# One core: W_in's low parts, token pieces and W_out's last block at other places of a scheduled three-layer kernel

## The chip, the cores and the metric

The kernel runs on one core of one Trainium2 chip, in one launch. The metric is the device time of one execution in microseconds (us). TensorE (PE) multiplies, VectorE (DVE), ScalarE (ACT) and GpSimd (POOL) prepare its operands and take up its results, and SyncE's queue (SP) issues every large transfer between HBM and the on-chip memory.

## The reference

Three stages, each feeding the next:

```python
# attention with decay, per head h of 8, batch 2, 768 tokens, head_dim 64
state = gamma * state + outer(k[t], v[t]);  y[t] = scale * q[t] @ state
# x = y as 1536 tokens x 512
# mixture: P from exp(x @ w_gate), 8 rounds of row and column normalization
for e in range(8): out += P[:, e:e+1] * (maximum(x @ w1[e], 0) @ w2[e])   # 512 -> 1024 -> 512
# dense layer on that output
h = x @ w_in;  g = maximum(h, 0) + alpha * minimum(h, 0);  y = g @ w_out   # 512 -> 2048 -> 512
```

## The kernel before, in words

**Phases.** After the attention, 20 phases follow, each one half of the tokens (768) with one expert or with one half of the dense layer's 2048 columns. Phases 0 to 7 are the first half's experts, 8 to 15 the second half's, 16 to 19 the dense layer (first half, columns' halves 0 and 1; second half, 1 and 0). In phases 8 to 19 ("fast", `FAST`) a phase is a list of 56 positions. Each position is one of the seven products of a Strassen scheme on one column block of four, and each is six matmuls of 384 columns: three for the first and three for the second half of the contraction. Positions 0 to 26 and 28 are nearly all layer 1 (x by W_in), the rest layer 2 (h by W_out). From position 27 on layer 2's products u = 0 to 27 follow.

**Three matmuls for one product.** Both operands stand as a high part (rounded to fp32r by ScalarE) and a low part (what the rounding lost, a subtraction). `mm3` (L313 to L315) multiplies high by high, high by low, low by high, in this order, and all accumulate in one bank. So the low part of an operand is wanted one matmul later than its high part.

**Where operands come from.** A block `n` of W_in (four for each phase, n = 4 * phase + j) is loaded raw from HBM (`w_load`, L124). POOL makes its four sums (`w1_sum`, L139). ScalarE makes the high part in three pieces a, c and b (`w1_high`, L162), VectorE the low part (`w1_low`, L172). The raw buffers are two: block n + 2 is loaded when block n's part b (at its low step) has been issued, which `w1_low` queues in `unkept`, to be issued two positions later. `w1_at` gives the positions of the adds and of the three high and low steps; its first numbers for blocks n + 4 and n + 5 belong to the phase after.
The hidden state of layer 2 has 14 parts (`hs`): for each, ScalarE writes the high part (L1072) and VectorE the low part (L1080, or L1050 with the relu, or L1052). Part k is first wanted at layer 2's product 2k.
W_out of a dense block is prepared once, one block in each of phases 8 to 15 (`dense_prep`): load `dr` (L270), high `dw` (L275), low (L279), sums on POOL (L289), high and low of the sums, stored to HBM (L298), from where `ws` pieces are loaded later (L1091).
The tokens of a half are kept as pieces `xs` in HBM (`x_keep`: a term on POOL, L374, the high part on ScalarE, L382, a low part on POOL, L386, a store, L389) and fetched (L394). x_keep(2, k) is the second half's tokens for the experts, x_keep(3, k) the second half's for the dense layer, made from `total`, the mixture's output.

**What sets the order.** `step(phase, position, fn)` appends a function that issues instructions behind that position's matmuls; a position of 60 or more means position - 60 of the next phase. Each engine runs its instructions in the order of issue, and waits for each of them to have its inputs; so a waiting instruction holds back everything behind it on its engine. SP's queue is one such order: a load that waits for a buffer holds back the loads behind it.

**Gathers.** POOL adds layer 2's results of a phase to `total` in the next one (L1130, eight per phase, at positions 2, 5, 8, 11 for phases 10 to 15; for phase 15 they run during phases 15 and 16).

Of the kernel before, what the change touches and what calls it, by code (L numbers as in the profile page):

```python
# [23 lines left out]
E, F = 8, 1024  # L24
# [5 lines left out]
NJ = NF // 2  # L30
# [17 lines left out]
def tile_kernel(ctx, tc, lead, qkT, kv, ctab, w_gate, w1, w2, w_in, w_out, alpha, out):  # L48
# [119 lines left out]
    def w1_low(n, part, eng):  # L168
        if n >= NJ * len(PHASES) or same(n) or n // NJ in AGAIN and part == "c":
            return  # L170
        lo, src, hi = ws1[n].pop(part)
        eng.tensor_tensor(out=lo, in0=src, in1=hi.bitcast(F32), op=ALU.subtract)  # L172
        if part == "b" and n not in (0, 2 * NJ * E - 2):
            if n < NJ * E:
                w_load(0, n + 2)
            else:
                unkept.append([2, w_load, 0, n + 2])
        if n < NJ * E and part != "a":
            unkept.append([2, w1_keep, n, part, hi, lo])
# [246 lines left out]
    with tc.manual_schedule():  # L426

        with ExitStack() as actx:
# [53 lines left out]
            pool, dve = nc.gpsimd, nc.vector  # L482
# [722 lines left out]
        pool, dve = nc.gpsimd, nc.vector  # L1205
# [20 lines left out]
        def step(ph, pos, *fns):  # L1226
            if pos >= 60:
                ph, pos = ph + 1, pos - 60
            for fn in fns:
                at(ph, seq[ph][pos], fn)  # L1230
# [20 lines left out]
        def w1_at(ph, m, add_eng, eng, adds, ah, al, ch, cl, bh, bl):  # L1251
            step(ph, adds, lambda: w1_adds(m, add_eng))
            for part, hi, lo in (("a", ah, al), ("c", ch, cl), ("b", bh, bl)):
                step(ph, hi, lambda part=part: w1_high(m, part))
                step(ph, lo, lambda part=part: w1_low(m, part, eng))
# [7 lines left out]
        xk, x3 = [], []  # L1263
        for ph in range(len(PHASES)):
# [28 lines left out]
            if fast:  # L1293
                w1_at(ph, n + 2, pool, dve, 0, 4, 5, 5, 7, 10, 11)
                w1_at(ph, n + 3, pool, dve, 5, 10, 12, 12, 14, 17, 18)
                w1_at(ph, n + 4, pool, dve, 28 if ph == 2 * E - 1 else 18, 36, 38, 39, 40, 42, 43)
                w1_at(
                    ph, n + 5, pool, dve, 36 if ph >= 2 * E else 28,
                    *((44, 51, 48, 53, 50, 55) if ph == 2 * E - 1 else (44, 45, 48, 49, 50, 52))
                )  # L1300
            else:
                if ph:
# [29 lines left out]
            if fast:  # L1332
# [6 lines left out]
                        step(ph, (2, 5, 8, 11)[q // 2], lambda m=q // 2, h=q % 2: gather(m, h))  # L1339
                if ph < 2 * E:  # L1340
                    step(ph, 0, lambda ph=ph: weight_load(ph))
                    for pos, fn in zip((6, 14, 24, 27, 40, 52), dense_prep(ph - E)):
                        step(ph, pos, fn)
                o = ph < 2 * E
                for pos, fn, jp in (
# [8 lines left out]
                    step(ph, lows[k], lambda ph=ph, k=k: hlow(ph, k))  # L1354
                for pos, jp in ((34 if o else 40, 0), (36 if o else 41, 1)):
                    step(ph, pos, lambda ph=ph, jp=jp: t4(ph, jp))
                if ph in (E + 1, E + 4):
                    step(ph, 0, lambda k=(ph - E - 1) // 3: xk.extend(x_keep(2, k, *x_load(2, k))))
                if ph == 2 * E:
                    for k in range(2):  # L1360
                        step(ph, 8 + k, lambda k=k: x3.append(x_keep(3, k, *x_copy(k, total))))
                    step(ph + 1, 39, lambda: new_x(3, B22, T4))
                    for i, keys in enumerate((
# [4 lines left out]
                    )):  # L1368
                        for q, to in enumerate(keys):
                            step(ph + to // 56, to % 56, lambda i=i, q=q: x3[i % 2][i // 2][q]())  # L1370
# [149 lines left out]
```

## Time and profile before

| | |
|---|---|
| median of 3 runs | 1263.19 us (1262.98 to 1263.47) |
| profiled execution | 1262.42 us |
| its span | 1260.3 us |
| TensorE busy | 1251.2 us, 99% of the span |
| VectorE, ScalarE, POOL busy | 1006.5, 653.0, 446.8 us |
| granted TensorE clock | 1.0 of full speed over the whole span |

The profiled execution is 0.8 us under the median, and 2.1 us of it lie around the span. Since TensorE is busy 99% of the span, the time can only be moved by the waits that remain between two of its matmuls. A fast phase without waits is 56 positions of six matmuls. The rows of a timeline say when an instruction started, how long it ran, its engine and line, and in brackets, for how long the engine had idled and what released it. A matmul of 384 columns is shown with some 0.33 us, and the starts of two that don't wait lie 0.17 us apart, since they overlap.

### The profile page before, as it was taken

How to read it: one execution, taken by the hardware profiler on the slowest of the kernel's cores; microseconds unless marked ns; L12 is line 12 of the kernel's file. 1: busy time of each engine (PE TensorE's matmuls, PEld its weight loads, DVE VectorE, ACT ScalarE, POOL GpSimd, SP SyncE). 2: the span in 40 equal slices, each digit the busy share in tenths (PEclk: the TensorE clock that was granted, in tenths of full speed). 3: DMA queues.
4: the chain of work that ended last, by engine and by line, in shares of the span. 5: the costliest groups of instructions: out<-in, count | busy, mean ns of one | idle time of the engine just before them, and what ended most of it. 6: DMA issues, size and time to landing. Idle time of an engine off the chain costs nothing.

```text
span 1260.3 us, 20491 instructions
## 1 busy us (share of the span) xinstructions
PE 1251.2 (99%) x7358; PEld 1189.4 (94%) x7358; DVE 1006.5 (80%) x1538; ACT 653.0 (52%) x1211; POOL 446.8 (35%) x408
## 2 busy tenths in 40 slices
PE   9999999999999999999999999999999999999998
PEld 7889999989898989899999999999999999999998
DVE  6677888888888888859696968787786999797866
ACT  5644534444444445456455454546464656655573
POOL 5733252526161616101033433142413464633110
PEclk9999999999999999999999999999999999999999
DMA  9884999999999999899988989898989976684616
GB/s 361 275 286 144 318 342 353 329 339 335 346 338 338 337 341 341 280 345 343 378 293 326 324 297 334 308 348 300 351 285 320 339 269 192 224 302 169 213 56 184
DMA packets 219990, 375.00 MB, mean 298 GB/s; under 512 B 15809, under 2 KB 133617, under 8 KB 219889
## 3 DMA queue, kind: packets, MB, share of 16 engines
q1 hardware_dynamic: 219888, 373.70, 87.0%
q8 instruction: 58, 0.95, 0.3%
q14 instruction: 44, 0.35, 0.1%
HBM read 240.97 MB, written 131.10 MB: 295 GB/s over the span
## 4 chain that ended last, share of the span: by engine, by line
PE 90%; DVE 6%; DMA 2%; issue 1%; ACT 1%; SPq 0%; DVEq 0%
PE B L314 7%; PE B L313 7%; PE B L315 7%; PE o L313 7%; PE o L315 7%; PE o L314 7%; PE A L313 6%; PE A L315 6%; PE A L314 6%; PE D L314 4%; PE D L315 4%; PE D L313 4%; PE E L315 4%; PE E L313 4%; PE E L314 4%; DVE hs L1080 1%
## 5 line engine op out<-in xcount | busy, mean ns | idle before, releaser
L1072 ACT ACTIVATE hs<-b 128x768 fp32r<-128x768 f32 x168 | 139.1, 841 | 65.5 <-DVE b L1046 22.4
L139 POOL TENSOR_TENSOR raw<-raw 128x256 f32<-128x256 f32 x128 | 124.9, 986 | 92.6 <-DMA raw<-wd 52.4
L1080 DVE TENSOR_TENSOR hs<-b,hs 128x768 fp32r<-128x768 f32 x120 | 122.8, 1028 | 14.9 <-ACT hs L1072 14.6
L246 POOL TENSOR_TENSOR pr<-pr 128x256 f32<-128x256 f32 x52 | 51.0, 982 | 188.7 <-ACT ex L872 62.7
L313 PE MATMUL A<-xh,W 128*128 128x384 f32 x320 | 107.8, 337 | 0.0
L315 PE MATMUL A<-xh,W 128*128 128x384 f32 x320 | 107.2, 335 | 0.0
L314 PE MATMUL A<-xl,W 128*128 128x384 f32 x320 | 107.0, 334 | 0.0
L162 ACT ACTIVATE W<-raw 128x512 fp32r<-128x512 f32 (+1 forms) x138 | 94.0, 695 | 19.2 <-DVE raw L139 19.2
L314 PE MATMUL B<-hs,ws 128*128 128x384 f32 x288 | 96.5, 335 | 2.4 <-DVE hs L1080 2.4
L313 PE MATMUL B<-hs,ws 128*128 128x384 f32 x288 | 96.3, 334 | 0.2 <-ACT W L162 0.2
L315 PE MATMUL B<-hs,ws 128*128 128x384 f32 x288 | 96.3, 334 | 0.0
L1130 POOL TENSOR_TENSOR total<-total,t 128x384 f32<-128x384 f32 x56 | 71.6, 1309 | 68.1 <-DVE t L1110 68.1
L979 DVE TENSOR_TENSOR b<-E,b 128x384 f32<-128x384 f32 x48 | 26.7, 556 | 84.2 <-ACT W L162 48.1
L386 POOL TENSOR_TENSOR xs<-b,xs 128x384 fp32r<-128x384 f32 x19 | 24.1, 1269 | 189.3 <-ACT xs L382 172.7
L313 PE MATMUL B<-xh,W 128*128 128x384 f32 x268 | 90.7, 338 | 0.0
L172 POOL TENSOR_TENSOR W<-raw,W 128x512 fp32r<-128x512 f32 (+1 forms) x49 | 76.1, 1566 | 40.0 <-PE B L315 22.9
L315 PE MATMUL B<-xh,W 128*128 128x384 f32 x268 | 89.7, 335 | 0.0
L314 PE MATMUL B<-xl,W 128*128 128x384 f32 x268 | 89.6, 334 | 0.0
L964 ACT ACTIVATE B<-A 128x384 f32<-128x384 f32 x48 | 22.8, 476 | 123.3 <-PE A L315 121.8
L289 POOL TENSOR_TENSOR dr<-dr 128x256 f32<-128x256 f32 x32 | 37.4, 1167 | 131.7 <-DVE dw L279 93.5
L172 DVE TENSOR_TENSOR W<-raw,W 128x512 fp32r<-128x512 f32 (+1 forms) x89 | 82.1, 939 | 1.1 <-ACT W L162 1.1
L313 PE MATMUL D<-xh,W 128*128 128x384 f32 x236 | 79.4, 336 | 0.0
(498 smaller groups left out, 3992.3 us busy)
## 6 DMA issues: line engine op xcount, KB each, us to landing
ws<-c SPq DMA_DIRECT2D x168, 512.0 KB, 5.8
raw<-in_w_dram SPq DMA_DIRECT2D x64, 512.0 KB, 5.6
c<-W SPq DMA_DIRECT2D x64, 384.0 KB, 6.6
W<-c SPq DMA_DIRECT2D x22, 768.0 KB, 7.7
pr<-in_w_dram SPq DMA_DIRECT2D x32, 512.0 KB, 6.0
c<-pw SPq DMA_DIRECT2D x32, 512.0 KB, 7.2
c<-pr SPq DMA_DIRECT2D x32, 512.0 KB, 7.8
raws<-in_w_dram SPq DMA_DIRECT2D x32, 384.0 KB, 6.3
```

The lines of the kernel that those rows point to most:

```text
L139: eng.tensor_tensor(out=out, in0=in0, in1=in1, op=op)
L162: nc.scalar.activation(out=hi, in_=src, func=AF.Copy)
L172: eng.tensor_tensor(out=lo, in0=src, in1=hi.bitcast(F32), op=ALU.subtract)
L246: eng.tensor_tensor(out=out, in0=in0, in1=in1, op=op)
L289: nc.gpsimd.tensor_tensor(out=out, in0=in0, in1=in1, op=op)
L313: nc.tensor.matmul(ps, ah, bh, start=first, stop=False, skip_group_check=True)
L314: nc.tensor.matmul(ps, ah, bl, start=False, stop=False, skip_group_check=True)
L315: nc.tensor.matmul(ps, alo, bh, start=False, stop=last, skip_group_check=True)
L979: nc.vector.tensor_tensor(out=dst, in0=src, in1=dst, op=ALU.add)
L1072: nc.scalar.activation(out=t[:, 0, :], in_=hsource(ph, k), func=func)
L1080: nc.vector.tensor_tensor(out=lo, in0=src, in1=hi.bitcast(F32), op=ALU.subtract)
L1130: eng.tensor_tensor(out=dst, in0=dst, in1=tt[m, h], op=ALU.add)
```

## The change

The full diff, of which the numbers are positions:

```diff
--- before.py
+++ after.py
@@ -170,7 +170,8 @@
             return
         lo, src, hi = ws1[n].pop(part)
         eng.tensor_tensor(out=lo, in0=src, in1=hi.bitcast(F32), op=ALU.subtract)
-        if part == "b" and n not in (0, 2 * NJ * E - 2):
+        last = "c" if n // NJ in (2 * E, 2 * E + 1) and n % NJ == 1 else "b"
+        if part == last and n not in (0, 2 * NJ * E - 2):
             if n < NJ * E:
                 w_load(0, n + 2)
             else:
@@ -1293,10 +1294,14 @@
             if fast:
                 w1_at(ph, n + 2, pool, dve, 0, 4, 5, 5, 7, 10, 11)
                 w1_at(ph, n + 3, pool, dve, 5, 10, 12, 12, 14, 17, 18)
-                w1_at(ph, n + 4, pool, dve, 28 if ph == 2 * E - 1 else 18, 36, 38, 39, 40, 42, 43)
+                late_lows = ph in (2 * E - 1, 2 * E)
                 w1_at(
-                    ph, n + 5, pool, dve, 36 if ph >= 2 * E else 28,
-                    *((44, 51, 48, 53, 50, 55) if ph == 2 * E - 1 else (44, 45, 48, 49, 50, 52))
+                    ph, n + 4, pool, dve, 28 if ph == 2 * E - 1 else 18,
+                    *((36, 51, 39, 52, 42, 53) if late_lows else (36, 38, 39, 40, 42, 43))
+                )
+                w1_at(
+                    ph, n + 5, pool, dve, 28,
+                    *((44, 55, 48, 60, 50, 54) if late_lows else (44, 45, 48, 49, 50, 52))
                 )
             else:
                 if ph:
@@ -1339,7 +1344,8 @@
                         step(ph, (2, 5, 8, 11)[q // 2], lambda m=q // 2, h=q % 2: gather(m, h))
                 if ph < 2 * E:
                     step(ph, 0, lambda ph=ph: weight_load(ph))
-                    for pos, fn in zip((6, 14, 24, 27, 40, 52), dense_prep(ph - E)):
+                    places = (6, 14, 24, 27, 40, 52) if ph < 2 * E - 1 else (2, 10, 18, 19, 36, 52)
+                    for pos, fn in zip(places, dense_prep(ph - E)):
                         step(ph, pos, fn)
                 o = ph < 2 * E
                 for pos, fn, jp in (
@@ -1354,17 +1360,18 @@
                     step(ph, lows[k], lambda ph=ph, k=k: hlow(ph, k))
                 for pos, jp in ((34 if o else 40, 0), (36 if o else 41, 1)):
                     step(ph, pos, lambda ph=ph, jp=jp: t4(ph, jp))
-                if ph in (E + 1, E + 4):
-                    step(ph, 0, lambda k=(ph - E - 1) // 3: xk.extend(x_keep(2, k, *x_load(2, k))))
+                if ph in (E + 1, E + 3):
+                    k = (ph - E) // 2
+                    step(ph, 40 * k, lambda k=k: xk.extend(x_keep(2, k, *x_load(2, k))))
                 if ph == 2 * E:
                     for k in range(2):
                         step(ph, 8 + k, lambda k=k: x3.append(x_keep(3, k, *x_copy(k, total))))
                     step(ph + 1, 39, lambda: new_x(3, B22, T4))
                     for i, keys in enumerate((
                         (16, 16, 17, 19), (17, 17, 17, 21), (38, 38, 39, 42), (42, 42, 43, 45),
-                        (44, 48, 49, 51), (50, 54, 55, 57), (54, 60, 61, 63), (60, 66, 67, 69),
-                        (66, 71, 72, 74), (70, 74, 75, 77), (97, 97, 98), (100, 100, 101),
-                        (96, 103, 104), (101, 107, 108),
+                        (44, 48, 49, 51), (52, 56, 57, 59), (57, 61, 62, 64), (61, 66, 67, 69),
+                        (66, 70, 71, 73), (69, 74, 75, 77), (106, 106, 107), (110, 110, 110),
+                        (107, 111, 112), (108, 113, 114),
                     )):
                         for q, to in enumerate(keys):
                             step(ph + to // 56, to % 56, lambda i=i, q=q: x3[i % 2][i // 2][q]())
```

In words: (1) In phases 15 and 16 the low parts of the next phase's first two W_in blocks (64, 65 and 68, 69) move behind layer 2's last low parts of h, to positions 51 to 55 and the next phase's position 0. (2) For blocks 65 and 69 the load of the block two further is now issued behind part c instead of b. (3) In phase 15 the steps of W_out's last block stand at 2, 10, 18, 19, 36, 52 instead of 6, 14, 24, 27, 40, 52. (4) The load of the second half's tokens, k = 1, moves from phase 12, position 0, to phase 11, position 40. (5) Most steps that make the second half's token pieces for the dense layer move some positions later, the last ones from phase 17, position 40 on to phase 17, position 50 on.

VectorE's order at the end of phase 15, before. `hs15_k` are the low parts of h, `W_144<-raw0_64` the low parts of W_in's block 64, `E2` and `t15` sums of layer 2's results, `dr7` the low part of W_out's last block:

```order
L1080 TENSOR_TENSOR hs15_8_10622<-b120_15_10309,hs15_8_10622 128x768
L1160 TENSOR_TENSOR E2_15_0_10640<-B2_15_0_10552,d2_15_0_10599 128x384
L172 TENSOR_TENSOR W_144<-raw0_64_10426,W_144 128x512
L1160 TENSOR_TENSOR E2_15_1_10656<-B2_15_1_10566,d2_15_1_10612 128x384
L1080 TENSOR_TENSOR hs15_9_10643<-b121_15_10475,hs15_9_10643 128x768
L172 TENSOR_TENSOR W_144<-raw0_64_10426,W_144 128x768
L1110 TENSOR_TENSOR t15_00_10685<-A2_15_0_10503,pb15_10216 128x384
L1050 SCALAR_TENSOR_TENSOR hs15_10_10677<-b220_15_10225,hs15_10_10677 128x768
L1110 TENSOR_TENSOR t15_10_10698<-A2_15_1_10535,pb15_10216 128x384
L172 TENSOR_TENSOR W_144<-raw0_64_10426,W_144 128x512
L1050 SCALAR_TENSOR_TENSOR hs15_11_10701<-b221_15_10391,hs15_11_10701 128x768
```

And there in the changed kernel, some rows further:

```order
L1081 TENSOR_TENSOR hs15_12_10736<-b210_15_10235,hs15_12_10736 128x768
L1111 TENSOR_TENSOR t15_01_10760<-E2_15_0_10641,pb15_10216 128x384
L1081 TENSOR_TENSOR hs15_13_10752<-b211_15_10375,hs15_13_10752 128x768
L1111 TENSOR_TENSOR t15_11_10770<-E2_15_1_10657,pb15_10216 128x384
L172 TENSOR_TENSOR W_144<-raw0_64_10431,W_144 128x512
L172 TENSOR_TENSOR W_144<-raw0_64_10431,W_144 128x768
L280 TENSOR_TENSOR dr7_10239<-dr7_10239,dw7_10325 128x1024
L172 TENSOR_TENSOR W_144<-raw0_64_10431,W_144 128x512
L1111 TENSOR_TENSOR t15_20_10797<-B2_15_0_10552,pb15_10216 128x384
L172 TENSOR_TENSOR W_144<-raw0_65_10437,W_144 128x512
L1111 TENSOR_TENSOR t15_30_10808<-B2_15_1_10566,pb15_10216 128x384
L172 TENSOR_TENSOR W_144<-raw0_65_10437,W_144 128x512
```

The three W_in rows that stood between `hs15_9` and `hs15_11` now stand behind `hs15_13`, all six of block 64 and 65 together with `dr7`.

SP's queue from the end of phase 16, before. `ws17` are pieces of W_out for phase 17, `raw0_70` and `raw0_71` blocks of W_in, `xc3<-xs3` stores of token pieces:

```order
L1091 DMA ws17_0_11345<-c2_9_121 128x2x512
L389 DMA xc3_123<-xs3_1_1_11315 128x2x384
L124 DMA raw0_70_11349<-wd0_6_131 128x1024
L1091 DMA ws17_1_11364<-c2_9_121 128x2x512
L1091 DMA ws17_2_11385<-c2_9_121 128x2x512
L1091 DMA ws17_3_11407<-c2_9_121 128x2x512
L389 DMA xc3_123<-xs3_0_4_11377 128x2x384
L1091 DMA ws17_4_11424<-c2_9_121 128x2x512
L124 DMA raw0_71_11436<-wd0_7_132 128x1024
L1091 DMA ws17_5_11444<-c2_9_121 128x2x512
```

And in the changed kernel:

```order
L1092 DMA ws17_0_11342<-c2_9_121 128x2x512
L390 DMA xc3_123<-xs3_1_1_11313 128x2x384
L1092 DMA ws17_1_11358<-c2_9_121 128x2x512
L1092 DMA ws17_2_11379<-c2_9_121 128x2x512
L1092 DMA ws17_3_11399<-c2_9_121 128x2x512
L390 DMA xc3_123<-xs3_0_4_11371 128x2x384
L1092 DMA ws17_4_11418<-c2_9_121 128x2x512
L1092 DMA ws17_5_11435<-c2_9_121 128x2x512
L124 DMA raw0_70_11439<-wd0_6_131 128x1024
L124 DMA raw0_71_11478<-wd0_7_132 128x1024
```

The load of `raw0_70` stood ahead of `ws17_1`, and stands now behind `ws17_5`.

POOL's order at the start of phase 17, before (`b0_3_0`, `ba_3_1` the token terms of L374, `xs3` their low parts, `raw0_70` the sums of a W_in block):

```order
L374 TENSOR_TENSOR ba_3_1_10936<-ba_3_1_10936 128x384
L374 TENSOR_TENSOR b0_3_0_10921<-b1_3_0_10922,b0_3_0_10921 128x384
L386 TENSOR_TENSOR xs3_1_4_11433<-ba_3_1_10936,xs3_1_4_11433 128x384
L139 TENSOR_TENSOR raw0_70_11349<-raw0_70_11349 128x256 x4
L374 TENSOR_TENSOR ba_3_1_10936<-bb_3_1_10937,ba_3_1_10936 128x384
L386 TENSOR_TENSOR xs3_0_5_11499<-b0_3_0_10921,xs3_0_5_11499 128x384
L139 TENSOR_TENSOR raw0_71_11436<-raw0_71_11436 128x256 x4
L374 TENSOR_TENSOR b0_3_0_10921<-b0_3_0_10921,b1_3_0_10922 128x384
```

And in the changed kernel:

```order
L375 TENSOR_TENSOR ba_3_1_10936<-ba_3_1_10936 128x384
L139 TENSOR_TENSOR raw0_70_11439<-raw0_70_11439 128x256 x4
L387 TENSOR_TENSOR xs3_1_4_11451<-ba_3_1_10936,xs3_1_4_11451 128x384
L375 TENSOR_TENSOR b0_3_0_10921<-b1_3_0_10922,b0_3_0_10921 128x384
L375 TENSOR_TENSOR ba_3_1_10936<-bb_3_1_10937,ba_3_1_10936 128x384
L139 TENSOR_TENSOR raw0_71_11478<-raw0_71_11478 128x256 x4
L387 TENSOR_TENSOR xs3_0_5_11510<-b0_3_0_10921,xs3_0_5_11510 128x384
L375 TENSOR_TENSOR b0_3_0_10921<-b0_3_0_10921,b1_3_0_10922 128x384
```

The sums of `raw0_70` and the wait for its load now stand ahead of `xs3_1_4` and of the term that `xs3_0_5` needs. In the kernel before they stood behind both.

## Rows read from the trace of the kernel before

**Rows 1.** PE's waits, whole span: operation and releaser: us in all, times, longest.

```profile
PE B L314 <- DVE hs L1080: 2.4, 3, 1.1
...
PE E L314 <- DVE hs L1050: 0.5, 1, 0.5
PE E L314 <- DVE hs L1052: 0.3, 1, 0.3
PE B L313 <- ACT W L162: 0.2, 1, 0.2
```

**Rows 2.** PE's timeline at the end of phase 16: start, us, engine, line, operation.

```profile
1074.53 0.33 PE L315 MATMUL E<-hs,ws 128*128 128x384 f32 x1
1074.71 0.34 PE L313 MATMUL B<-hs,ws 128*128 128x384 f32 x1
1076.15 0.45 PE L314 MATMUL B<-hs,ws 128*128 128x384 f32 x1 [1.11 <-DVE hs L1080]
```

**Rows 3.** Chain that ends at 803 us, in phase 12: start, us, what.

```profile
789.51 10.96 DMA dr<-wd
```

**Rows 4.** PE's timeline in phase 12.

```profile
801.58 0.34 PE L315 MATMUL D<-xh,W 128*128 128x384 f32 x1
801.99 0.45 PE L313 MATMUL E<-xh,W 128*128 128x384 f32 x1
```

**Rows 5.** VectorE's timeline at the end of phase 15.

```profile
1009.64 1.03 DVE L172 TENSOR_TENSOR W<-raw,W 128x512 fp32r<-128x512 f32 x1
1010.60 1.76 DVE L1050 SCALAR_TENSOR_TENSOR hs<-b,hs 128x768 fp32r<-128x768 f32 x1
```

**Rows 6.** VectorE's timeline in the middle of phase 15.

```profile
981.65 0.95 DVE L1080 TENSOR_TENSOR hs<-b,hs 128x768 fp32r<-128x768 f32 x1
...
988.23 2.43 DVE L1080 TENSOR_TENSOR hs<-b,hs 128x768 fp32r<-128x768 f32 x2
990.58 1.49 DVE L1046 TENSOR_TENSOR b<-b,b 128x768 f32<-128x768 f32 x1
```

**Rows 7.** POOL's timeline, phases 15 to 17.

```profile
986.28 4.97 POOL L289 TENSOR_TENSOR dr<-dr 128x256 f32<-128x256 f32 x4 [23.12 <-DMA xh<-xc]
...
1018.95 4.99 POOL L139 TENSOR_TENSOR raw<-raw 128x256 f32<-128x256 f32 x4
1023.89 4.38 POOL L1130 TENSOR_TENSOR total<-total,t 128x384 f32<-128x384 f32 x4
...
1081.37 3.06 POOL L139 TENSOR_TENSOR raw<-raw 128x256 f32<-128x256 f32 x4
```

**Rows 8.** PE's timeline: matmuls of phases 15, 16 and 17.

```profile
990.39 0.33 PE L314 MATMUL A<-hs,ws 128*128 128x384 f32 x1
...
1030.99 0.33 PE L313 MATMUL E<-xh,W 128*128 128x384 f32 x1
...
1091.72 0.33 PE L313 MATMUL E<-xh,W 128*128 128x384 f32 x1
```

**Rows 9.** DMA from 1008 to 1032 us: transfers, KB each, median us to landing.

```profile
raw<-wd SPq DMA_DIRECT2D x2, 512.0 KB, 4.5
...
c<-dr SPq DMA_DIRECT2D x1, 512.0 KB, 3.1
```

**Rows 10.** ACT's timeline at the starts of phases 16 and 17.

```profile
1028.13 0.58 ACT L935 ACTIVATE n<-A,sa 128x384 f32<-128x384 f32 x1 [0.41 <-PE A L315]
...
1029.12 0.48 ACT L964 ACTIVATE E<-B 128x384 f32<-128x384 f32 x1
...
1085.12 0.51 ACT L382 ACTIVATE xs<-b 128x384 fp32r<-128x384 f32 x1
...
1089.90 0.47 ACT L964 ACTIVATE E<-B 128x384 f32<-128x384 f32 x1
```

**Rows 11.** SP's timeline at the start of phase 17.

```profile
1080.45 0.36 SPq L1091 DMA_DIRECT2D ws<-c  x1
```

**Rows 12.** DMA from 1070 to 1090 us.

```profile
raw<-wd SPq DMA_DIRECT2D x2, 512.0 KB, 6.3
```

## The prediction, on record before the changed kernel ran

> **What bounds the kernel now.** I read the page's engine shares first, then the list of TensorE's waits, then the timelines of the engines around the few waits that it names. TensorE is busy for 99% of the span, at a granted clock of 1.0 (the 2.4 GHz level) in every slice, and the change leaves its matmuls and their order as they are. So the change is worth what it takes from, or adds to, the gaps between matmuls. The reader is to see how few gaps there are: behind VectorE's low parts of h three of 2.4 us together, one of 0.5 and one of 0.3, and behind ScalarE's W_in part one of 0.2 [rows 1]. The list counts a little less than a gap costs. At the end of phase 16 the starts lie 1.44 us apart, where 0.18 would do, so the gap costs about 1.26 there and is listed with 1.11; the matmul behind it starts late by another tenth [rows 2]. I add 0.27 to each listed gap for that.
>
> All these gaps are together 3.4 us listed, about 5 us with the additions. That is the most the change can win from them.
>
> **The change part by part.** Every sum is made against the profiled execution, 1262.42 us (span 1260.3 and 2.1 around it), which lies 0.8 us under the median of 1263.19; I add the difference that comes out to the median.
>
> (a) The token load moved from phase 12 to phase 11. In phase 12 the load of W_out's block is 10.96 us on its way [rows 3], behind the two token loads on the same queue. ScalarE then converts that block in front of the copy that TensorE's next product needs, and that product starts 0.41 us behind the one before instead of 0.18 [rows 4]; with the tenth behind it, 0.35. Without the two loads the block comes earlier: -0.4. If phase 11, position 40, is as crowded, nothing is won; it can't cost more than the same 0.4 there, so the bounds are -0.4 and +0.4.
>
> (b) W_out's last block earlier in phase 15. The load, the high and the low part stand before the product that needs anything of them; the load at position 2 is covered by the eight positions to 10. I take 0; if the load were as slow as in phase 12 (10.96 us against 8 positions of 1.04 us [rows 3]), ScalarE would stand for some 2.6 us, of which the copies behind it hide most; upper bound +0.8, an estimate.
>
> (c) Its sums at position 19 instead of 27. They hold POOL for 4.97 us from 986.28, and POOL's sums of W_in follow without a gap [rows 7]. They start when VectorE's low part of that block is done, and that moves from position 24 to 18, about 5 us. So POOL is now busy from some 981 on, over five more microseconds in which VectorE works on low parts that TensorE waits for next. A 768-wide VectorE operation took 0.95 us at 981.65, with POOL idle, and 1.49 at 990.58, with POOL busy [rows 6]. I count nine VectorE operations with both inputs in the on-chip memory that come to lie beside POOL, at 0.54 each: 4.9. Of this 1.2 comes back, since the low part of W_out's block (1.2 us) has left this place, and two low parts have slack of about 1.0 (the one that ends about 989.4 is needed at 990.39 [rows 6, 8]) and 0.8. That leaves +1.9. If only the operations as wide as in the row count, six of the nine, 3.2 - 1.2 - 1.8 leaves +0.2; if the slack is half, it is +2.8. I take 1.9, since the nine come from the order of the engine, one by one.
>
> (d) W_in's low parts of block 64 out of phase 15's second half. One of them, 1.03 us at 1009.64, stands right in front of a low part of h which itself takes 1.76 [rows 5]. TensorE's wait for it, and the next one, are the 0.5 and one of the three of L1080; the other two of these hold 1.3 together beside the longest, 1.1 [rows 1, 2], so 0.65. The 0.2 behind ScalarE lies there too. With 0.27 each: 0.77 + 0.92 + 0.47 = 2.2. VectorE has then only low parts and gathers to make: -2.2 (at best that, at worst 0 if POOL's collisions alone make them late).
>
> (e) The start of phase 16. The low parts now stand behind h's last low part, then the low part of W_out's block, then block 64's part b, and only then may block 66 be loaded. From the last of h's parts the five VectorE operations end about 1.1 us into phase 16 (4.6 us by the widths, begun 3.5 us before it; an estimate). Then the load takes 4.5 us by the median of this stretch [rows 9], POOL's sums 3.1 when alone [rows 7], and three of the four gathers behind them 3.3 (4.38 for four [rows 7]). ScalarE's sign step at 1028.13 needs the third gather's buffer, and the copy at 1029.12, which follows on the same engine, needs 1.5 us from there [rows 10]. 1.1 + 4.5 + 3.1 + 3.3 + 1.5 = 13.5 us into the phase. TensorE wants that copy at its twelfth position, 1030.99 [rows 8], 11.5 into the phase: +2.0. In the kernel before, POOL had the load in time: its sums begin at 1018.95 without a wait [rows 7]. Behind the waiting sums on POOL stand the gathers, and behind ScalarE's high part of that block the copies for the second column block: both engines wait in one place. With the fastest large transfer of this stretch, 3.1 [rows 9], it is +0.6; with the loads of the next phase, 6.3 [rows 12], and sums of 4.1 instead of 3.1, +4.8.
>
> The Trainium skill, page "DMA: Bandwidth & Descriptors", section "Anatomy of one DMA — SWDGE (gpsimd) path", gives 2.0 us and the bytes at 436 GB/s for one transfer: 3.2 us for 512 KB, an estimate. The stretch shows 4.5 for these loads, so the measurement decides; by the rule (e) would be +0.7 and (g) +0.1, nearly the fast rival below.
>
> (f) Blocks 68 and 69 likewise out of phase 16's second half: the longest wait, 1.1, and the 0.3 [rows 1, 2], with 0.27 each: 1.95, so -1.9. At worst 0.
>
> (g) The start of phase 17. The load of block 70 now stands behind the piece of W_out that SP issues at 1080.45, 0.2 us into the phase [rows 11], so it starts some 0.65 into it and lands 6.3 later [rows 12]. POOL's sums for it, 3.1 [rows 7], now stand ahead of a low token part (1.0) and of the term (1.0) that ScalarE's token step at 1085.12 needs; from there to the end of the copy at 1089.90 ScalarE needs some 2.7 of its own work [rows 10]. 0.65 + 6.3 + 3.1 + 2.0 + 2.7 = 14.7 into the phase, wanted at 11.5 (1091.72 [rows 8]): +3.2. With 3.1 for the load it is +0.1, with POOL's sums at 4.1 it is +4.3.
>
> (h) The last token pieces go behind the low parts of phase 17's end, so POOL is quiet beside these: the last of the three waits, 0.65 and 0.27: -0.9 (worst 0). They are due in phase 18 only.
>
> Sum: -0.4 + 0 + 1.9 - 2.2 + 2.0 - 1.9 + 3.2 - 0.9 = +1.7. The profiled execution would be 1264.1, the median 1264.9. A measurement of this kernel tells no change from a change below about 0.2%, 2.5 us, so this forecast is "no change".
>
> **The rivals.**
>
> Fast loads: the transfers land in 3.1 us. For it: that is what a 512 KB transfer in this stretch took [rows 9]. Against it: the loads of W_in themselves took 4.5 and 6.3 [rows 9, 12]. Then (e) is +0.6, (g) +0.1 and (c) at its lower end +0.2: -0.4 + 0.2 - 2.2 + 0.6 - 1.9 + 0.1 - 0.9 = -4.5, 1258.7.
>
> Slow loads: the loads of 66 and 70 take 6.3, and POOL's sums beside VectorE's low parts 4.1, so that (e) is +4.8 and (g) +4.3: -0.4 + 1.9 - 2.2 + 4.8 - 1.9 + 4.3 - 0.9 = +5.6, 1268.8. For it: sums of 4.99 at 1018.95 [rows 7], and the low parts moved to just this place. Against it: 4.5 in that stretch. It decides from about 5 us for (e): each further microsecond of a load is one of time in both places.
>
> The waits at the ends of phases 15 and 16 stay: the change moves the low parts, but ScalarE's high parts or POOL's sums make h late anyway, so that (d) and (f) give half. For it: the low part of h took 1.76 where the same work alone takes 0.95 [rows 5, 6], POOL or not. Against it: VectorE has 2.7 us less to do there. Then +1.7 + 2.05 = +3.8, 1267.0.
>
> **How the numbers follow.** Forecast 0.40, fast loads 0.30, slow loads 0.20, waits stay 0.10. The forecast case reaches some 2.5 us both ways, which spills about as much over either edge of 0.2%. Faster than 1260.7: 0.30 in all; slower than 1265.7: 0.20 + 0.10 of the rivals, and 0.02 more; so 0.30, 0.38 and 0.32. The forecast alone has a range of 1262.4 to 1267.4. As cases on both sides hold half, the range goes to the fast rival's value less a little, 1258.4, and to 1268.4 above, since the slow one is 0.20 and half of it lies below that.
>
> **What would show it.** In the changed profile: in the list of waits the three for L1080, and the 0.5 and 0.3, are gone ((d), (f), (h)). In place of them stand waits of products 9 to 12 of phases 16 and 17 for ScalarE's copies, 2 and 3 us (e, g), POOL's sums of blocks 66 and 70 begin late, behind a wait for their load, and phase 15 has waits of low parts near its middle (c). If phases 16 and 17 start without such waits, (e) and (g) are wrong, and the time is under 1261. If the waits for L1080 are still there, (d) and (f) are.

## The result and the profile after

The changed kernel takes 1271.83 us (median of 6 runs, 1271.15 to 1272.83), the one before 1263.2 (6 runs, 1261.32 to 1264.24): a ratio of 1.0071, interval 1.0058 to 1.0084. It is 8.6 us slower. Forecast were 1264.9 and a range of 1258.4 to 1268.4.

Where the time went is seen best by phase. This table gives the microseconds from the first matmul of a phase to that of the next, in one profiled execution of each kernel; without a wait it is 58.3 to 58.4.

| phase | before | changed | lows alone (e5) | pieces alone (e6) | W_out's block alone (e7) |
|---|---|---|---|---|---|
| 12 | 59.12 | 58.45 | 59.97 | 58.45 | 59.04 |
| 15 | 60.65 | 61.20 | 58.92 | 60.63 | 60.35 |
| 16 | 60.73 | 64.87 | 66.15 | 59.53 | 60.75 |
| 17 | 59.63 | 64.49 | 62.62 | 58.66 | 59.63 |
| 18 | 58.33 | 58.33 | 58.33 | 58.33 | 58.33 |

From phase 12 to 17 that is -0.67 + 0.55 + 4.14 + 4.86 = +8.9. Outside the span the changed kernel's executions take 1.8 us and those of before 2.1, which leaves some 8.5, and 8.6 was measured. (The start of phase 8 lies anywhere between 546.6 and 548.3 us in the executions of these kernels, whichever it is; that is no part of the change, and it makes 1.6 of the 10.4 us between the two profiled executions, 1262.42 and 1272.83.) Phase 15 varies too: up to its end e1, e4 and e9 below have the code of the changed kernel, and it takes 60.62, 61.67 and 60.34 there against 61.20 here. Its +0.55 is one of four such values.

TensorE's waits of the changed kernel, all of 0.2 us and more from phase 15 on (operation, releaser: us in all, times, longest):

```profile
PE E L314 <- ACT E L965: 6.3, 2, 3.4
PE A L314 <- ACT B L965: 2.2, 3, 1.0
PE E L314 <- DVE b L980: 0.8, 1, 0.8
PE D L315 <- DVE hs L1081: 0.6, 1, 0.6
```

The waits of before for low parts of h at the ends of phases 15 to 17 [rows 1] are off this list. The ones of 0.8 and 0.6 are new, in phase 15's middle, and one of the three for B copies is in phase 15 too, at 975. The rest are ScalarE's copies, which make TensorE wait at positions 7 and 11 of phases 16 and 17. And there is a second loss right behind the long ones. TensorE's timeline of phase 16 at position 11:

```profile
1033.30 0.34 PE L316 MATMUL D<-xh,W 128*128 128x384 f32 x1
1037.03 0.69 PE L314 MATMUL E<-xh,W 128*128 128x384 f32 x1 [3.39 <-ACT E L965]
1037.52 0.52 PE L315 MATMUL E<-xl,W 128*128 128x384 f32 x1
...
1039.76 0.51 PE L316 MATMUL A<-xh,W 128*128 128x384 f32 x1
1040.08 0.36 PE L314 MATMUL A<-xh,W 128*128 128x384 f32 x1
1040.28 0.34 PE L315 MATMUL A<-xl,W 128*128 128x384 f32 x1
```

The first matmul waits 3.4 us, and those behind it start 0.32 us apart instead of 0.17. Here is the same stretch, with the wait behind it and that of phase 17, by windows (stretch: length, busy us of each engine with its instructions, granted clock, DMA share, GB/s):

```profile
1034.00:1037.00 3.00, 0.00 (x0) 0.00 (x0) 0.87 (x2) 1.49 (x4) 3.00 (x4) 0.95 0.12 46
1037.00:1040.00 3.00, 2.97 (x9) 2.97 (x10) 1.72 (x4) 3.00 (x6) 2.47 (x4) 0.50 0.95 271
1040.00:1045.00 5.00, 5.00 (x30) 5.00 (x30) 4.29 (x7) 3.61 (x7) 0.00 (x0) 0.99 1.05 406
...
1101.70:1104.70 3.00, 2.96 (x9) 2.96 (x10) 2.03 (x5) 3.00 (x7) 2.92 (x4) 0.50 0.01 3
```

The granted clock is 0.50, the level of 1.2 GHz, for the three microseconds behind each of the two long waits (3.4 and 2.9 us), and 0.99 again behind them. Nine matmuls at 0.32 instead of 0.17 are 1.3 us, 1.5 with the start.

What makes ScalarE late is the chain that step (e) followed. SP issues block 66's load, POOL waits for it and then does its sums, the gathers stand behind the sums, and ScalarE's sign step behind the third gather:

```profile
1022.34 0.32 SPq L124 DMA_DIRECT2D raw<-wd  x1
```

```profile
1028.19 3.70 POOL L139 TENSOR_TENSOR raw<-raw 128x256 f32<-128x256 f32 x4 [8.48 <-DMA raw<-wd]
1031.85 4.58 POOL L1131 TENSOR_TENSOR total<-total,t 128x384 f32<-128x384 f32 x4
...
1093.37 3.72 POOL L139 TENSOR_TENSOR raw<-raw 128x256 f32<-128x256 f32 x4 [11.62 <-DMA raw<-wd]
1097.06 1.02 POOL L387 TENSOR_TENSOR xs<-ba,xs 128x384 fp32r<-128x384 f32 x1
1098.04 1.01 POOL L375 TENSOR_TENSOR b<-b,b 128x384 f32<-128x384 f32 x1
```

```profile
1028.12 0.63 ACT L162 ACTIVATE W<-raw 128x512 fp32r<-128x512 f32 x1 [2.08 <-DMA raw<-wd]
...
1035.51 0.58 ACT L936 ACTIVATE n<-A,sa 128x384 f32<-128x384 f32 x1 [3.56 <-POOL total L1131]
...
1036.50 0.48 ACT L965 ACTIVATE E<-B 128x384 f32<-128x384 f32 x1
...
1099.08 0.52 ACT L383 ACTIVATE xs<-b 128x384 fp32r<-128x384 f32 x1 [4.21 <-POOL b L375]
...
1101.21 0.48 ACT L965 ACTIVATE E<-B 128x384 f32<-128x384 f32 x1
```

Phase 16 begins at 1021.01. Block 66's load is issued 1.3 us into it and is there 7.0 us into it, about 5.7 later; in the kernel before POOL had no wait at this place [rows 7]. The copy that TensorE waits for ends 16.0 us into the phase, where 11.5 was wanted. The high part of block 66 at 1028.12 holds the copy behind it as well, which is the smaller wait of about 0.7 listed at position 7 (and 1.0 in phase 17). In phase 17 (from 1085.88) POOL's order is the one that the change makes: sums of block 70, low part, term, and ScalarE's token step at 1099.08 waits 4.21 us for that term. Its copy ends 15.8 us into the phase.

### The profile page after: what moved, and what is told of

It is laid out like the page before. It is cut to its first block, busy times and chain, and to the rows that moved or that the text cites. A ratio compares the mean times of both kernels' runs of the same rounds, so it can differ in the third digit from the quotient of the medians.

```text
span 1271.1 us, 20491 instructions
## 1 busy us (share of the span) xinstructions
PE 1255.6 (99%) x7358; PEld 1193.8 (94%) x7358; DVE 1001.2 (79%) x1538; ACT 652.6 (51%) x1211; POOL 440.9 (35%) x408
## 4 chain that ended last, share of the span: by engine, by line
PE 91%; DVE 4%; DMA 2%; POOL 1%; ACT 1%; issue 1%; SPq 0%; POOLq 0%; DVEq 0%
PE B L314 7%; PE B L316 7%; PE B L315 7%; PE o L314 7%; PE o L316 7%; PE o L315 7%; PE A L314 6%; PE A L315 6%; PE A L316 6%; PE E L314 4%; PE E L316 4%; PE E L315 4%; PE D L315 4%; PE D L316 4%; PE D L314 4%; PE y L598 1%
## 5 line engine op out<-in xcount | busy, mean ns | idle before, releaser
L139 POOL TENSOR_TENSOR raw<-raw 128x256 f32<-128x256 f32 x128 | 119.2, 941 | 103.7 <-DMA raw<-wd 64.1
L247 POOL TENSOR_TENSOR pr<-pr 128x256 f32<-128x256 f32 x52 | 51.4, 988 | 189.3 <-DMA pr<-in_w_dram 61.9
L314 PE MATMUL E<-xh,W 128*128 128x384 f32 x216 | 73.6, 341 | 7.1 <-ACT E L965 6.3
```

Source lines behind the costliest of these rows:

```text
L139: eng.tensor_tensor(out=out, in0=in0, in1=in1, op=op)
L247: eng.tensor_tensor(out=out, in0=in0, in1=in1, op=op)
L314: nc.tensor.matmul(ps, ah, bh, start=first, stop=False, skip_group_check=True)
```

## Experiments

All are timed against the kernel before, which gave 1263.1 to 1263.5 in their company. The changed kernel's 1271.83 is from runs on another occasion; a median's difference below about 1 us is not read.

**e1: TensorE kept busy in the two long waits.** The product of position 10 is computed four times in phase 16 and three times in phase 17.

```diff
-            for k in range(2):
+            more = {2 * E: 3, 2 * E + 1: 2}.get(ph, 0) if (j, p) == (1, 7) else 0
+            for k in [0, 1] * more + [0, 1]:
```

> The changed kernel, in which TensorE computes position 10's product of phase 16 four times and that of phase 17 three times (the last one counts), so that it is busy for 3.1 and 2.1 us of the two long waits at position 11. Theory (the slow matmuls behind the two waits, 0.32 us apart, come from the granted clock, which falls when TensorE stands for 3 us): the matmuls behind both waits stand 0.17 us apart, and the time falls by some 2.5 to 2.9 us, to about 1269.1. Rival (they are slow for another reason, such as low parts or weights that come late behind the wait): no change, 1271.8, or slower by what is computed twice beyond the waits.

Measured: 1271.49 us, ratio 1.0064 (1.0047 to 1.0080). TensorE at position 11 of phase 16, and the granted clock there:

```profile
1035.47 0.34 PE L316 MATMUL D<-xh,W 128*128 128x384 f32 x1
1036.13 0.44 PE L314 MATMUL E<-xh,W 128*128 128x384 f32 x1 [0.32 <-ACT E L966]
1036.41 0.34 PE L315 MATMUL E<-xl,W 128*128 128x384 f32 x1
```

```profile
1034.00:1037.00 3.00, 2.68 (x16) 2.36 (x15) 1.44 (x3) 2.40 (x6) 2.92 (x4) 1.00 0.43 131
1037.00:1040.00 3.00, 3.00 (x18) 2.68 (x17) 3.00 (x5) 3.00 (x7) 2.23 (x3) 1.00 0.96 307
```

The mechanism is as the theory has it: the clock stays at 1.00 and the matmuls lie 0.17 us apart. But its price is not: the time moves by 0.3 us, where 2.5 to 2.9 were expected. The repeated products have taken most of the wait for E copies, 1.6 now for 6.3, but there is one wait more among these, and for B copies 3.8 where it had 2.2:

```profile
PE A L314 <- ACT B L966: 3.8, 4, 1.8
PE E L314 <- ACT E L966: 1.6, 3, 0.8
```

In phase 16 the load came 0.3 us later in this execution than in that of the changed kernel. Even so the three products behind the wait are done 0.9 us earlier (19.8 instead of 20.7 into the phase), so the slow clock cost about 1.2 us there, the sum of the two as an estimate. In phase 17 the load came 0.8 us later, and what the clock had cost there can't be told; part of what was gained is lost to waits of 0.4 and 0.5 for later copies, which the changed kernel doesn't have. That the repeated products finish position 10 some 3 us later is not the reason: ScalarE's copy of it, at 1036.83, waits for nothing. So the clock's price in the whole time stays open. In e4, e5 and e9 the executions with the lowest mean clock are the slowest ones (e5: 1271.55 and 1271.1 at 0.997, 1268.4 and 1269.55 at 0.999 and 1.0), but a longer wait would make both.

**e2: W_in's low parts back.** The rest as changed; the edit is the diff's first and second part undone. (With it goes a move that the words on the change leave out: the sums of block n + 5 at 28 instead of 36 from phase 16 on. e3 keeps it.)

```diff
-        if part == last and n not in (0, 2 * NJ * E - 2):
+        if part == "b" and n not in (0, 2 * NJ * E - 2):
...
-                late_lows = ph in (2 * E - 1, 2 * E)
+                    ph, n + 5, pool, dve, 36 if ph >= 2 * E else 28,
+                    *((44, 51, 48, 53, 50, 55) if ph == 2 * E - 1 else (44, 45, 48, 49, 50, 52))
```

> The changed kernel with W_in's low parts of phases 15 and 16 where they were before, the rest as changed. Theory (the late low parts make the raw loads of blocks 66 and 70 late, and these make both long waits): the waits at positions 7 and 11 of phases 16 and 17 go, with the slow matmuls behind them (4.8 + 4.4 + 2.9 us), and the waits at the ends of phases 15 and 16 come back (2.2 + 1.8): 1271.8 - 8.1 = 1263.7. Rival (phase 17's wait is from the token pieces' later steps, which stand ahead on ScalarE): only phase 16 recovers, 1271.8 - 4.8 - 1.5 + 4.0 = 1269.5.

Measured: 1261.56 us, 0.9983 (0.9974 to 0.9993). The late low parts make the waits of both phases, and the pieces' order alone doesn't. The kernel is faster than the theory had it, since the waits at the ends don't come back with the low parts:

```profile
PE B L314 <- DVE hs L1080: 0.8, 1, 0.8
...
PE D L314 <- DVE hs L1080: 0.6, 1, 0.6
```

The 0.5 for L1050 [rows 1] is gone, and of the three for L1080's B products, 2.4, one of 0.8 is left, at the end of phase 16. Phase 16 is now 60.86 long, phase 17 58.66.

**e3: only one block of each pair late.**

```diff
-                    *((36, 51, 39, 52, 42, 53) if late_lows else (36, 38, 39, 40, 42, 43))
+                    36, 38, 39, 40, 42, 43
```

> The changed kernel with the low parts of the first block of each pair (64, 68) back at positions 38, 40, 43, so that blocks 66 and 70 can be loaded early; those of 65 and 69 stay late. Theory (only the first block's low parts hold back the load that makes the wait): the waits at the starts of phases 16 and 17 go (12.1 us with the slow matmuls), those at the ends come back in part (2.2 in phase 15, 0.9 in phase 16): about 1262.8. Rival (block 65's and 69's late low parts, or ScalarE's order, make it): waits of 2 us or more stay at position 11, 1266 or more.

Measured: 1261.08 us, 0.9977 (0.9967 to 0.9986). The first block's low parts alone hold back the load that matters. No wait for ScalarE's E copies is left; one of 0.4 for a B copy stays, in phase 15. Phase 16 is 59.30.

```profile
PE A L314 <- ACT B L965: 0.4, 1, 0.4
```

**e4: block 66's sums behind the gathers.** One gather still follows the sums, and the load is no earlier than in the changed kernel.

```diff
-                w1_at(ph, n + 2, pool, dve, 0, 4, 5, 5, 7, 10, 11)
+                w1_at(ph, n + 2, pool, dve, 4 if ph == 2 * E else 0, 4, 5, 5, 7, 10, 11)
```

> The changed kernel with POOL's sums of block 66 behind the last four gathers of phase 15 instead of ahead of them (issued at position 4 of phase 16 instead of 0). The load is as late as in the changed kernel. Theory (at phase 16's position 11 the wait is for the gathers that stand on POOL behind the late block's sums; the load alone costs the wait at position 7): position 11's wait falls from 3.9 to under 1 us, the matmuls behind it keep 0.17, 1271.8 - 4.9 = 1266.9. Rival (the load is the price, since ScalarE stands for block 66's high part anyway): no change, 1271.8.

Measured: 1268.89 us, 1.0041 (1.0026 to 1.0056). Phase 16 is 60.67 instead of 64.87. POOL and ScalarE there:

```profile
1024.40 1.39 POOL L1131 TENSOR_TENSOR total<-total,t 128x384 f32<-128x384 f32 x1 [1.10 <-DVE t L1111]
1028.62 3.73 POOL L139 TENSOR_TENSOR raw<-raw 128x256 f32<-128x256 f32 x4 [2.83 <-DMA raw<-wd]
```

```profile
1031.56 0.85 ACT L162 ACTIVATE W<-raw 128x768 fp32r<-128x768 f32 x1 [1.45 <-POOL raw L139]
1032.32 0.56 ACT L936 ACTIVATE n<-A,sa 128x384 f32<-128x384 f32 x1
```

The load lands 0.5 us later into the phase than in the changed kernel (issued 1.7 us later, it took 4.6), and the sums begin that much later, but the sign step now follows the high part at once and no longer waits 3.56 us for a gather. So most of phase 16's wait at position 11 was the gathers' place behind a waiting instruction on POOL. The 4.2 us in the phase are less than the theory's 4.9 and more than the 2.9 by which the medians differ; phases 15 and 17 were 0.5 and 0.3 longer in this execution.

**e5: W_in's low parts alone, on the kernel before.** The edit is the diff's first and second part, nothing else.

```diff
+                late_lows = ph in (2 * E - 1, 2 * E)
...
+                    *((36, 51, 39, 52, 42, 53) if late_lows else (36, 38, 39, 40, 42, 43))
...
+                    *((44, 55, 48, 60, 50, 54) if late_lows else (44, 45, 48, 49, 50, 52))
```

> The kernel before with W_in's low parts and the load behind part c as in the changed kernel, and nothing else of the change. Theory formed after the first four runs (the late low parts bring the waits at the starts of phases 16 and 17, and win nothing at the ends of phases 15 and 16, where POOL's sums and token pieces beside them make the low parts of h late): the waits of 0.79 and 0.88 near the end of phase 15 and of 0.54 and 1.38 of phase 16 stay, and the time is 6 us (phase 16) and 3 us (phase 17, where the token steps are still ahead of the late block) over before: 1272. Rival (the prediction's steps (d) and (f)): these waits go, 4.1 us, and the time is 1268.

Measured: 1270.32 us, 1.0057 (1.0042 to 1.0072).

```profile
PE E L314 <- ACT E L965: 3.4, 1, 3.4
PE A L314 <- ACT B L965: 2.9, 4, 1.0
PE B L315 <- DVE hs L1081: 1.0, 1, 1.0
```

The theory falls in one half: the low parts do win at the ends. Phase 15 gets shorter, 58.92 instead of 60.65, and its two waits at the end go, as do the 0.3 and the 1.1 of phase 16, as steps (d) and (f) had it. The late loads cost at least what the changed kernel shows, so they cost more than all that is won. Phase 16, 66.15, is 1.3 longer than there: behind the same wait of 3.4 us sixteen matmuls lie 0.32 us apart here, at a granted clock of 0.50 from 1036.4 to 1041.8, where the changed kernel has nine.

**e6: the token pieces alone, on the kernel before.**

```diff
-                        (44, 48, 49, 51), (50, 54, 55, 57), (54, 60, 61, 63), (60, 66, 67, 69),
+                        (44, 48, 49, 51), (52, 56, 57, 59), (57, 61, 62, 64), (61, 66, 67, 69),
...
-                        (96, 103, 104), (101, 107, 108),
+                        (107, 111, 112), (108, 113, 114),
```

> The kernel before with only the later steps of the second half's token pieces. Theory (these steps on POOL, beside the low parts of h, make the 1.38 wait at the end of phase 16 and the 0.96 at the end of phase 17): both go, 1261.0. Rival (the W_in low parts in front of them make the first): only the one of phase 17 goes, 1262.3.

Measured: 1261.62 us, 0.9987 (0.9978 to 0.9997).

```profile
PE B L314 <- DVE hs L1080: 0.6, 1, 0.6
```

In the profiled execution, the fastest of the ten (1260.1), the longest wait of before, 1.11 listed at the end of phase 16 [rows 2], is gone with the pieces alone, and so is that of phase 17. The first holds for this execution only: in e2, with the same pieces, 0.84 of it stays. The difference lies in VectorE's second low part at L1052, first in e6, then in e2:

```profile
1070.89 0.94 DVE L1052 TENSOR_TENSOR hs<-b,hs 128x768 fp32r<-128x768 f32 x1
```

```profile
1072.20 1.77 DVE L1052 TENSOR_TENSOR hs<-b,hs 128x768 fp32r<-128x768 f32 x1
```

Both begin 51.5 us into the phase, which starts at 1019.36 in e6 and at 1020.69 in e2. POOL's token step begins 51.4 us into it in e2 (1072.10), beside the low part, and 52.9 in e6 (1072.28), behind it. ScalarE's step in front of it waits for a store of a piece, issued 44.9 us into the phase in both, which took 5.8 us in e2 and 7.4 in e6. So W_in's low parts in front are part of the cause (e5 takes the wait away by moving them), and whether the token step meets a low part hangs on one store.

**e7: W_out's last block alone, on the kernel before.**

```diff
-                    for pos, fn in zip((6, 14, 24, 27, 40, 52), dense_prep(ph - E)):
+                    places = (6, 14, 24, 27, 40, 52) if ph < 2 * E - 1 else (2, 10, 18, 19, 36, 52)
+                    for pos, fn in zip(places, dense_prep(ph - E)):
```

> The kernel before with only W_out's last block at positions 2, 10, 18, 19, 36, 52 of phase 15. Theory (POOL's sums, five microseconds earlier, meet the low parts in the middle of the phase instead of those at its end): 2.7 us of waits come in the middle, at about 974, 989 and 997, and the 2.2 us at the end go: 1263.8. Rival (prediction's step (c), with the waits at the end due to W_in's low parts, which stay here): 1265.2 or more.

Measured: 1263.33 us, 1.0003 (0.9994 to 1.0013). Waits at 974, 989 and 996 us, 0.3, 0.2 and 0.5 in the list, stand for the two at the end of phase 15, which are gone: 60.35 instead of 60.65.

```profile
PE B L314 <- DVE hs L1080: 1.8, 2, 1.1
PE D L314 <- DVE hs L1080: 0.5, 1, 0.5
PE A L313 <- ACT B L964: 0.3, 1, 0.3
...
PE E L313 <- DVE b L979: 0.2, 1, 0.2
```

The 1.8 is in phases 16 and 17.

**e8: e3 with W_out's block where it was before.** The edit is shown against e3.

```diff
-                    places = (6, 14, 24, 27, 40, 52) if ph < 2 * E - 1 else (2, 10, 18, 19, 36, 52)
-                    for pos, fn in zip(places, dense_prep(ph - E)):
+                    for pos, fn in zip((6, 14, 24, 27, 40, 52), dense_prep(ph - E)):
```

> The kernel with 64's and 68's low parts early and 65's and 69's late, and W_out's last block at its places before; the tokens and the pieces as changed. Theory (the block's earlier sums move waits from the end of phase 15 to its middle and win nothing): phase 15 is as long as in the kernel with the earlier sums, within 0.4 us, so 1261.1 within 0.5. Rival (the middle waits are the price and those at the end are kept away by 65's late low parts): phase 15 falls to 58.6, 1259.3.

Measured: 1260.34 us, 0.9977 (0.9968 to 0.9987). Phase 15 is 60.66 here and 60.42 in e3, so the block's place moves the waits and wins or loses nothing that can be told.

**e9: two token pieces' steps back, in the changed kernel.**

```diff
-                        (44, 48, 49, 51), (52, 56, 57, 59), (57, 61, 62, 64), (61, 66, 67, 69),
+                        (44, 48, 49, 51), (50, 54, 55, 57), (54, 60, 61, 63), (61, 66, 67, 69),
```

> The changed kernel with the steps of two token pieces (the fifth and sixth lists of positions) where they were before, so that on POOL the term for ScalarE's token step stands ahead of block 70's sums again. Block 70 is loaded as late as in the changed kernel. Theory (phase 17's wait at position 11 is partly POOL's: low part and term behind the late sums, 2.0 us, and ScalarE behind them; the wait at position 7 is the load alone): position 7 still waits 1.2, position 11 waits 0.7 to 1.2 instead of 3.4, and phase 17 falls from 64.5 to some 61.5; 1268.9. Rival (the late load is the price whatever stands behind it): phase 17 stays at 64 or more, 1271.8.

Measured: 1269.5 us, 1.0049 (1.0032 to 1.0066). Phase 17 is 62.11 instead of 64.49. The wait at position 11 is gone altogether. ScalarE there:

```profile
1095.54 0.85 ACT L162 ACTIVATE W<-raw 128x768 fp32r<-128x768 f32 x1 [1.45 <-POOL raw L139]
1096.29 0.56 ACT L936 ACTIVATE n<-A,sa 128x384 f32<-128x384 f32 x1
...
1097.26 0.48 ACT L965 ACTIVATE E<-B 128x384 f32<-128x384 f32 x1
```

No token step waits ahead of the sign step. The 2.4 us of the phase hold the slow clock too, which doesn't come here: the longest wait of the phase is 1.8. What is left is the load's own price: 1.8 at position 7 (the load took longer than in the changed kernel's profile), and two later waits of 0.6 for B copies.

**e10: e3 with the sums at 21.** The edit is shown against e3.

```diff
-                    places = (6, 14, 24, 27, 40, 52) if ph < 2 * E - 1 else (2, 10, 18, 19, 36, 52)
+                    places = (6, 14, 24, 27, 40, 52) if ph < 2 * E - 1 else (6, 14, 20, 21, 36, 52)
```

> The kernel with blocks 64's and 68's low parts early and 65's and 69's late, and W_out's last block at 6, 14, 20, 21, 36, 52, between the places of before and of the changed kernel. Theory (the sums only move the waits of phase 15 between its middle and its end; the wait at 974 is from ScalarE's conversion at position 10 alone): no wait at 974, about 1.5 us of others, phase 15 at 60.0 and the time at 1260.0. Rival (POOL's five microseconds meet both ends): phase 15 at 61 or more, 1261.0 or more.

Measured: 1259.47 us, 0.9970 (0.9958 to 0.9982); phase 15 is 60.01, without a wait at 974.

```profile
PE D L315 <- DVE hs L1081: 0.5, 1, 0.5
PE B L315 <- DVE hs L1081: 0.4, 1, 0.4
PE E L315 <- DVE hs L1053: 0.3, 1, 0.3
```

This is the best version: 3.7 us faster than the kernel before and 12.4 than the changed one. It keeps the token load, the token pieces and the second block's late low parts, and gives up the first block's. Phase 16 is 59.33 long, phase 17 58.66. Its lead over e3 and e8 is within their intervals.

Not tried: a third raw buffer for blocks 66 and 70, which would let all low parts be late and the loads early.

## Why the prediction was wrong

It was wrong in size: +1.7 was forecast, called no change, and +8.6 came. The steps that failed are (e) and (g), the loads at the starts of phases 16 and 17. Their chains were the right ones, link by link; the terms were too small by 4.0 and 2.9, for loads and sums that took longer and for the low clock behind the waits, which no term had.

(a) Forecast -0.4, measured -0.67 in phase 12. All kernels with the moved load have 58.43 to 58.47 there; those without have 59.12, 59.97, 58.45 and 59.04. Right, with a price that differs from execution to execution.

(b), (c) and (d), phase 15: forecast 0 + 1.9 - 2.2 = -0.3, measured +0.55. (c) came out to the tenth in this execution: two waits in the middle, which end at 990.8 and 998.2, of 1.1 and 0.9 by the starts. That was in part luck. The first is 0.79 in the list here and in e4, and 0.22 in e1 and e9, which have the same code there; what differs is one VectorE instruction beside POOL's sums, L865, of 0.99 us here and in e4 and 0.42 in e1 and e9. And for nine lengthenings of 0.54 the rows have eight of 0.36 to 0.57 and some small ones, 4.0 in all for 4.9. (b) was wrong by 0.8, its upper bound, but not for the bound's reason, a late load: ScalarE's conversion at position 10 waits for nothing, and stands in front of a copy that TensorE waits for at 974; the copy waits no more in e10, where the conversion is at 14. (d)'s gain is there, but it was not (d)'s alone. With the block at its old places the low parts' move makes phase 15 1.73 us shorter (e5). With the block early the difference is 0.17 (61.20 against 61.37 in e2), which is less than phase 15 varies by itself; in e7 the early sums alone take the same waits away and bring their own. The Trainium skill, page "SBUF — State Buffer", section "Who interferes with whom", has VectorE and GpSimd exclude each other for operations that use the shared ports. This fits the rows of the middle of phase 15: VectorE's step at L868 took 1.11 us at 984.01 in the changed kernel, beside POOL's sums, and 0.69 where POOL was idle, at 967.17.

```profile
967.17 0.69 DVE L868 SCALAR_TENSOR_TENSOR a<-rd,a 128x512 f32<-128x512 uint32 x1
...
982.99 0.99 DVE L865 TENSOR_SCALAR a<-rd 128x512 uint32<-128x512 uint32 x1
984.01 1.11 DVE L868 SCALAR_TENSOR_TENSOR a<-rd,a 128x512 f32<-128x512 uint32 x1
```

(e) Forecast +2.0. The change in phase 16 is +4.14, and 1.9 were won there by (f), so (e) cost 6.0: about 4.5 of waits and 1.5 by the low clock. The first of the two failed numbers is the load's: I took the median of the stretch, 4.5 [rows 9], and the load took 5.7. The two loads behind that median took 3.8, before phase 16 began, and 5.1, issued 3.8 us into it among W_out's pieces; the second was the nearer neighbour. That the store and the pieces on the queue make the load longer is likely, but no run shows it. Sums of 3.7 instead of 3.1, 0.2 for the issue and 0.3 at the gathers make nearly all the rest of the 2.5 by which the chain was longer (16.0 into the phase against 13.5). The DMA view of the changed kernel from 1015 to 1042 us:

```profile
raw<-wd SPq DMA_DIRECT2D x3, 512.0 KB, 5.7
```

The Trainium skill, page "DMA: Bandwidth & Descriptors", section "Anatomy of one DMA — SWDGE (gpsimd) path", would give 3.2 us, an estimate, by a fit for transfers that GpSimd issues. These are issued by SyncE and took 5.7; the measurement decides. The rival built on fast loads is refuted. The second failed number is the clock, of which the prediction had nothing: 1.5 in this phase, of which e1 shows about 1.2.

(f) and (h) Forecast -1.9 and -0.9, and about that was won. The waits at the ends of phases 16 and 17 are gone; one of 0.14 earlier in phase 16, which the kernel before has as well, stays. Again two edits share a gain: the low parts alone take the waits at the end of phase 16 away (e5), and the pieces alone did so with the longest of them in e6, though not in all of e2. In e2, e6 and e7 phase 16 has no long wait at its start, with the loads of 66 and 70 in time.

(g) Forecast +3.2. Phase 17 is 4.86 longer, with 1.25 won at its end and near its start, so it cost 6.1: waits of 1.0 and 2.9 in the list, 4.7 by the starts of the matmuls, and the rest the low clock. The chain ends 15.8 us into the phase, against 14.7: the load took 6.7 instead of 6.3, the sums 3.7 instead of 3.1. e9 shows that the order of POOL and ScalarE, the low part and the term behind the late sums, was worth 2.4 of it, the low clock included.

Among the rivals, "slow loads" came nearest. Its +4.8 and +4.3 are near the waits that came, 4.5 and 4.7, and the 3.0 that its 1268.8 lacks are about the slow matmuls of the profiled execution. Its condition, loads that take longer than 5 us, was met by both. I had put 0.20 on it; the row of phase 17's loads, 6.3 [rows 12], was already in the trace, and I used it for (g) only.

## What to carry to other kernels

A step moved behind the critical work moves everything that it triggers: here a low part's end frees the buffer of the next block's load, and the load's end was the late thing. When an instruction that waits for a transfer stands in an in-order queue, count what stands behind it, and price the transfer with the slowest of its neighbours, not with their median. When two edits each remove the same wait, their gains don't add; run each alone before running both.

## What the runs showed of the hardware that was not expected

Behind waits of TensorE of 3.4 and 2.9 us the granted clock was 0.50 (1.2 GHz) for about three microseconds in the changed kernel, with matmuls 0.32 us apart, and so it was behind the 2.9 of e4. Behind the 3.4 of e5 it was 0.50 for 5.4 us of matmuls, so waits of the same length had different prices behind them. Behind waits of 1.0 us in the changed kernel and of 1.8 in e1 the matmuls lay 0.17 to 0.18 apart, from the second on, and with the long wait filled by repeated products (e1) the clock stayed at 1.00. One VectorE instruction, L865, took 0.99 us in three of the executions (the changed kernel, e2, e4) and 0.42 in the others, beside the same sums of POOL in e1 and e9.
